# Float64 weight conversion in three VectorE passes; all weight splits on VectorE

## The chip, the cores and the metric

The kernel runs on one core of a Trainium2 chip. The core has TensorE (PE: matmuls into PSUM), VectorE (DVE), ScalarE (ACT), GpSimd (POOL) and SyncE (SP, which here only issues DMAs). Each engine works through its own instructions in order, and semaphores tie the engines together. The metric is device microseconds of one execution; the time of a kernel is the median of its runs.

## The reference

Three stages follow each other on 2304 tokens of width 512. The first is attention with a threshold (4 batches, 8 heads, 576 positions, head width 64). The second is a mixture of eight experts in which each token goes to one expert. The third is a dense layer of width 2048:

```python
def _moe_ref(x, modality_id, w_gate, modality_bias, w1, w2):
    ...
    for e in range(E):                      # E = 8, w1 [8,512,1024], w2 [8,1024,512], float32
        mask = e_idx == e
        h = np.maximum(x[mask] @ w1[e], 0.0)
        out[mask] = gate_w[mask, None] * (h @ w2[e])

def _moe2_ref(x, w_in, w_out):              # w_in [512,2048], w_out [2048,512], float64
    h = x @ w_in
    g = np.maximum(0.01 * h, h)
    return (g @ w_out).astype(np.float32)
```

Only `w_in` and `w_out` matter for the edit itself. They arrive as float64 and the engines compute in float32, so the kernel rebuilds each float32 from the two 32-bit words of a float64. The low word is word 0 of a pair, the high word (sign, exponent, upper mantissa) word 1.

## The kernel before

**Exact products from split operands.** A float32 matrix product is made of three matmuls in a faster format: every operand is split into a high part and the remainder (`hh`, `hl` for activations, `w_3h`, `w_3l` for weights), and high×high, low×high and high×low are added up in PSUM. So each weight block of 128x1024 is split once (`wsplit`, line 1103): ACT copies the rounded high part, and then DVE or POOL subtracts it from the raw block. The argument `on_pool` says which of the two. Before, three of every four splits of expert weights went to POOL, and every second split of the dense layers' weights.

**The expert stage.** The tokens of an expert are gathered in units of 306. Eight units run in a loop (`for u in range(NSTAT)`, line 1362). Unit 0 reads weights called `we`, units 1 to 7 read `w0` to `w6`. A unit has eight steps `g1` (12 matmuls each of 306 columns: one 128-row block of the hidden layer), then eight steps `g2t` (12 matmuls each), and two transposes of the next unit's rows in between. After each `g1` step, ACT writes `hh` (line 1169) and DVE writes `hl` (line 1170) from the step's PSUM tile. Four PSUM tiles (`ps_a`) take turns, so `g1` step f+4 cannot begin before `hl` of step f has been written.

**What fills the steps.** Everything else is hung on steps by the lists `fills[i]`. It is recorded right after step i's matmuls, and it keeps that order on each engine. Splits of the unit's own second-layer weights stand at steps 0, 2, 4, 6 (`SB`), those of the next unit's first-layer weights at 10, 12, 14, 16 (`SA`). A split also lets SP issue the load of the block four splits ahead. The gathers of the unit after next stand at step 13 on POOL.

**Conversions.** There are 16 blocks to convert (`Convert`, line 1114), each 128x1024 values, worked as two halves of 128x512. Each has three parts, `a`, `b` and `c`, placed at steps by `CONV` (line 258): one block in unit 1, three in units 2, 4 and 7, two in units 3, 5 and 6. Part `a` takes the absolute value and clamps (two DVE instructions per half). Part `b` shifts and joins the words (two on DVE) and adds 1 on POOL (integer add). Part `c` shifts back and restores the sign (two on DVE). The first eight blocks are `wi`, the others `cvt`; the raw words are `cv`.

**Dense stage.** It follows after a branch that every engine passes (line 1425). It runs over 9 token blocks of 256. During the first block the last four splits of `wi` and the eight of `wd` (the converted `w_out`, stored to memory and read back) are made, and each `g1` step needs ACT, DVE (line 1175), ACT and DVE (line 1180) after it.

Of the kernel before, what the change touches and what calls it, by code (L numbers as in the profile page):

```python
# [262 lines left out]
HOTS = 0, 2, 4, 6, 8, 10  # L263
# [647 lines left out]
def tile_main(tc, q, k, v, tau, mod, w_gate, bias, w1, w2, w_in, w_out, out):  # L911
    nc = tc.nc
    P = 128
# [4 lines left out]
    V = nc.vector  # L918
    with ExitStack() as ctx:
        c = ctx.enter_context(tc.tile_pool(name="c", bufs=1))  # L920
# [9 lines left out]
        wd = dr.tile([8, P, 1024], F32, name="wd")  # L930
# [17 lines left out]
        onei = c.tile([P, 1], I32, name="onei")  # L948
# [39 lines left out]
        def rest3(_):  # L988
            nc.gpsimd.memset(lst8, 1.0)
            nc.gpsimd.affine_select(out=lst8, in_=lst8, pattern=[[1, 8], [-1, 8]], compare_op=ALU.is_ge, fill=0.0, base=0, channel_multiplier=0)  # L990
            nc.gpsimd.memset(tri, 1.0)
            nc.gpsimd.affine_select(out=tri, in_=tri, pattern=[[1, P]], compare_op=ALU.is_gt, fill=0.0, base=0, channel_multiplier=-1)
            nc.gpsimd.memset(ones, 1.0)
            nc.gpsimd.memset(onei, 1)

        def rest4(_):
            m32 = mod.bitcast(I32).rearrange("(n two) -> n two", two=2)
# [32 lines left out]
        AB, RB, RP, CB = 24, 5, 3, 6  # L1030
        gathers, raws = [], []

        def row_tile(nm):
# [59 lines left out]
        def wtile(nm, tag, dt=F32R):  # L1093
            return (x_tag[0] if tag == "n" else w_p).tile([P, 1024], dt, tag=f"w{tag}", name=nm, bufs=8)
# [12 lines left out]
            return wh, wl  # L1107

        THR_LO = struct.unpack("f", struct.pack("I", 0x38000000))[0]
        THR_HI = struct.unpack("f", struct.pack("I", 0x47EFFFFF))[0]  # L1110

        w_in_f = []

        class Convert:


            def __init__(self, n):
                self.ns = (2 * n, 2 * n + 1)

            def load(self):  # L1120
                self.r, self.t = [], []
                for n in self.ns:
                    ch, hf = divmod(n, 2)
                    raw = cv_p.tile([P, 1024], I32, tag="cvr", name=f"cv{n}", bufs=CB)
                    if ch < 8:
                        src = w_in.bitcast(I32).rearrange("(c p) f -> p c f", p=P)[:, 2 * hf:2 * hf + 2, ch * 512:(ch + 1) * 512]
                        nc.sync.dma_start(out=raw.rearrange("p (c f) -> p c f", c=2), in_=src)
                    else:
                        r0 = ((ch - 8) * 2 + hf) * P
                        nc.sync.dma_start(out=raw, in_=w_out.bitcast(I32)[r0:r0 + P, :])  # L1130
                    self.r.append(raw.rearrange("p (n w) -> p n w", w=2))

            def a(self):
                for n, r in zip(self.ns, self.r):
                    ch, hf = divmod(n, 2)
                    if ch < 8:
                        if hf == 0:
                            w_in_f.append(wtile(f"wi{ch}", "i", F32))
                        t = w_in_f[ch].bitcast(I32)[:, hf * 512:(hf + 1) * 512]
                    else:  # L1140
                        t = cv_p.tile([P, 512], I32, tag="cvt", name=f"cvt{n}", bufs=4)
                    self.t.append(t)
# [12 lines left out]
            def c(self):  # L1155
                for t in self.t:
                    V.tensor_scalar(out=t, in0=t, scalar1=1, scalar2=None, op0=ALU.logical_shift_right)
                for n, t, r in zip(self.ns, self.t, self.r):
                    V.scalar_tensor_tensor(out=t, in0=r[:, :, 1], scalar=-2147483648, in1=t, op0=ALU.bitwise_and, op1=ALU.bitwise_or)
                    ch, hf = divmod(n, 2)  # L1160
                    if ch >= 8:
                        later(6, lambda t=t, ch=ch, hf=hf: nc.sync.dma_start(out=wd[ch - 8, :, hf * 512:(hf + 1) * 512], in_=t.bitcast(F32)))
# [97 lines left out]
        def later(n, fn):  # L1260
            late.append([n, fn])
# [49 lines left out]
        hots = [cv_p.tile([P, 1024], I32, tag="cvr", name=f"hot{k}", bufs=CB) for k in range(3)]  # L1311
        hot_l = [t.bitcast(BF16)[:, 0:9 * P].rearrange("p (j q) -> p j q", q=P) for t in hots[0:2]]
        hot_h = hots[2].bitcast(F16)[:, 0:324].rearrange("p (j q) -> p j q", q=18)
        hot_v = hots[2].bitcast(F16)[:, 324:1620].rearrange("p (j v q) -> p j v q", v=4, q=18)
# [47 lines left out]
        for u in range(NSTAT):  # L1362
# [4 lines left out]
            if u == 0:  # L1367
                for i, fs in LATE.items():
                    for part, a, b in fs:
                        fills[i].extend(chain[part][a:b] if isinstance(chain[part], list) else [chain[part]])  # L1370
                for k, i in enumerate(S0):
                    fills[i].append(lambda k=k: first_w.split(k % 4 != 2))
                for i in range(2):
                    fills[LATE_ROWS[i]].append(lambda i=i: rows.update({i + 1: unit_rows(i)}))
                tr_at = LATE_TR
            else:
                for k, i in enumerate(SB):
                    fills[i].append(lambda k=k: wts[u].split(k % 4 != 2))
                if u == 1:
                    for i, f in zip(HOTS, (lambda: pos_low(0), lambda: pos_low(1), pos_high, lambda: pos_values(0), lambda: pos_values(1))):  # L1380
                        fills[i].append(f)
                    fills[HOTS[5]].append(lambda: step(pos_tables))
                    fills[HOTS[5] + 1].extend(c.load for c in convs[1:CB // 2])
            if not last:
                for k, i in enumerate(SA):
                    fills[i].append(lambda k=k: w_nxt.split(k % 4 != 2))
            if u:
                for ia, ib, ic in CONV.get(u, STG):
                    if cv < 16:
                        c = convs[cv]  # L1390
                        nx = convs[cv + CB // 2] if cv + CB // 2 < 16 else None
# [132 lines left out]
```

## Time and profile before

| what | value |
|---|---|
| median of 3 runs | 1100.1 us (1099.07 to 1100.85) |
| the profiled execution: its time, its span | 1096.98 us, 1095.3 us |
| busy PE, DVE, ACT, POOL over the span | 94%, 68%, 50%, 47% |
| eight expert units | 383.6 to 665.6 us of the span |
| first token block of the dense stage | 673.8 to 704.3 us |
| dense stage, the other eight blocks | until 1078 us |

The profiled execution ran 3.1 us below the median, and its span leaves out 1.7 us of its own time. All times of rows are counted from the start of the span. "Busy" is the time in which an engine has an instruction running, and that includes the time in which the instruction itself is held up. PEclk is the granted clock of TensorE as a share of full speed (2.4 GHz); 0.5 is the lower level, 1.2 GHz.

### The profile page before, as it was taken

Reading aid. Unit: us, or ns where it says so; the run is one execution under the profiler, and the core shown is the slowest. Engines: PE = TensorE matmul, PEld = TensorE weight load, DVE = VectorE, ACT = ScalarE, POOL = GpSimd, SP = SyncE. Lnnn points to the kernel's source line nnn. Section 1 sums busy time; section 2 is a strip of 40 time slices with the busy share of each in tenths; the row PEclk is TensorE's granted clock in tenths of the full one; section 3 lists DMA queues with packets and bytes.
Section 4 is the critical chain, followed back from the end, with each engine's and each line's share of the span. In section 5 each row is a group of like instructions: output and inputs, shape, how many; then the busy total and the mean of one; then the engine's idle time right before and its main releaser. Section 6 shows DMA issues by size and latency. Waiting matters only on the chain. (4 is left out here: it accounts for less than half of the span.)

```text
span 1095.3 us, 19110 instructions
## 1 busy us (share of the span) xinstructions
PE 1025.3 (94%) x6914; PEld 930.6 (85%) x6914; DVE 750.1 (68%) x1525; ACT 546.6 (50%) x1191; POOL 516.2 (47%) x461
## 2 busy tenths in 40 slices
PE   7999999999998889888879877899999999999997
PEld 4788998898897689888879876798989989899896
DVE  7999999999999599699999997822414224132240
ACT  4888888888886244434344334532313324133240
POOL 6688788777876558667777764400000000000000
PEclk9999999999999889989999988999999999999999
DMA  5322324334231285968777843510010100000000
GB/s 132 105 57 59 102 63 99 82 85 100 57 89 23 88 275 157 302 203 241 213 233 255 275 133 117 154 39 30 11 39 1 40 29 11 20 1 20 10 11 20
DMA packets 96264, 109.12 MB, mean 100 GB/s; under 512 B 34448, under 2 KB 74384, under 8 KB 96160
## 3 DMA queue, kind: packets, MB, share of 16 engines
q1 hardware_dynamic: 90880, 98.06, 30.1%
q0 software_dynamic: 5280, 9.75, 2.9%
q8 instruction: 56, 0.92, 0.3%
q14 instruction: 48, 0.39, 0.1%
HBM read 78.47 MB, written 19.96 MB: 90 GB/s over the span
## 5 line engine op out<-in xcount | busy, mean ns | idle before, releaser
L1465 POOL DMA_INDIRECT out<-yo,prow x18 | 17.3, 963 | 366.1 <-ACT yo L1252 366.1
L1175 DVE TENSOR_TENSOR g<-h,g 128x256 f32<-128x256 f32 x144 | 61.0, 424 | 171.7 <-ACT g L1174 171.7
L328 POOL TENSOR_TENSOR Pl<-rw,Ph 128x384 fp32r<-128x384 f32 x115 | 114.5, 1008 | 22.0 <-ACT Ph L323 18.0
L433 ACT ACTIVATE e<-s,mx 128x576 f32<-128x576 f32 x144 | 105.9, 745 | 22.9 <-DVE mx L425 21.7
L425 DVE TENSOR_REDUCE mx<-s 128x1 f32<-128x576 f32 x144 | 106.7, 750 | 14.0 <-PE s L420 10.2
L1174 ACT ACTIVATE g<-h 128x256 f32<-128x256 f32 x144 | 55.4, 385 | 107.0 <-PE h L1215 101.3
L447 DVE SCALAR_TENSOR_TENSOR pp<-s,tb,e 128x576 f32<-128x576 f32 x128 | 102.3, 807 | 4.6 <-ACT e L433 0.7
L1252 ACT ACTIVATE yo<-y,pgate 128x512 f32<-128x512 f32 x18 | 12.4, 688 | 169.8 <-PE y L1233 169.8
L466 PE MATMUL t<-ident,pp 128*128 128x128 f32 x576 | 89.4, 277 | 1.1 <-ACT rw L323 1.0
L420 PE MATMUL s<-kt,qt 128*128 128x288 f32 x256 | 80.5, 330 | 5.4 <-DVE pp L447 2.8
L490 POOL TENSOR_TENSOR Ph<-rw,zz 128x384 fp32r<-128x384 f32 x76 | 76.8, 1010 | 7.1 <-ACT rw L323 5.2
L560 PE MATMUL o<-Ph,hv 128*128 128x320 f32 (+3 forms) x237 | 75.4, 330 | 0.0
L420 PE MATMUL s<-k,qt 128*128 128x288 f32 x256 | 72.2, 296 | 0.0
L466 PEld LDWEIGHTS t<-ident,pp 128*128 128x128 f32 x576 | 67.0, 143 | 4.3 <-ACT rw L323 1.4
L1359 DVE TENSOR_TENSOR xl<-x,xh 128x256 fp32r<-128x256 f32 x36 | 13.0, 421 | 83.8 <-ACT xh L1358 83.8
L561 PE MATMUL o<-Pl,hv 128*128 128x320 f32 (+3 forms) x237 | 68.1, 299 | 0.2 <-POOL Pl L328 0.2
L1169 ACT ACTIVATE hh<-h 128x306 fp32r<-128x306 f32 x64 | 27.2, 427 | 71.2 <-PE h L1215 69.9
L429 DVE TENSOR_TENSOR tb<-mx,taub 128x1 f32<-128x1 f32 x144 | 60.8, 423 | 1.2
L323 ACT ACTIVATE rw<-t 128x384 f32<-128x384 f32 x111 | 54.8, 496 | 10.9 <-PE t L466 10.8
L1252 ACT ACTIVATE yo<-y 128x306 f32<-128x306 f32 x32 | 13.7, 428 | 88.4 <-issue 56.1
L420 PEld LDWEIGHTS s<-kt,qt 128*128 128x128 f32 x256 | 48.6, 190 | 9.3 <-issue 4.1
L560 PEld LDWEIGHTS o<-Ph,hv 128*128 128x128 f32 x237 | 44.9, 189 | 12.2 <-issue 11.9
(591 smaller groups left out, 3681.9 us busy)
## 6 DMA issues: line engine op xcount, KB each, us to landing
k<-kt SPq DMA_DIRECT2D x30, 304.0 KB
cv<-in_moe_w_in SPq DMA_DIRECT2D x16, 512.0 KB
cv<-in_moe_w_out SPq DMA_DIRECT2D x16, 512.0 KB
yt<-yo SPq DMA_DIRECT2D x32, 153.0 KB
x<-yt SPq DMA_DIRECT2D x9, 512.0 KB
rk<-in_k SPq DMA_DIRECT2D x16, 256.0 KB
rq<-in_q SPq DMA_DIRECT2D x16, 256.0 KB
rv<-in_v SPq DMA_DIRECT2D x16, 256.0 KB
```

Of the source, the lines that this page charges most:

```text
L328: fn.tensor_tensor(out=out, in0=a, in1=b.bitcast(F32), op=ALU.subtract)
L420: T.matmul(ps[:, j, 0:288], a, c, start=(m == 0), stop=(m == len(ops) - 1))
L425: V.tensor_reduce(out=mx, in_=get(g, f"s{s}"), op=ALU.min, axis=AX.XY)
L429: V.tensor_tensor(out=tb, in0=get(g, f"mx{s}"), in1=taub, op=ALU.add)
L433: A.activation(out=e, in_=get(g, f"s{s}"), func=AF.Exp, bias=get(g, f"mx{s}"), scale=-1.0)
L447: V.scalar_tensor_tensor(out=p.rearrange("p (a b) -> p a b", a=2), in0=get(g, f"s{s}"), scalar=get(g, f"tb{s}"), in1=get(g, f"e{s}"), op0= ...
L466: T.transpose(ps[:, m * P:(m + 1) * P], p[:, o:o + P], ident)
L490: G.tensor_tensor(out=hi, in0=rw, in1=zz.rearrange("p (a b) -> p a b", a=3), op=ALU.add)
L560: T.matmul(ps[:, a:b], V2[:, vb, :], hi[:, n, a:b], start=(c == 4), stop=False)
L561: T.matmul(ps[:, a:b], V2[:, vb, :], lo[:, n, a:b], start=False, stop=(c == 3))
L1174: nc.scalar.activation(out=g, in_=ps, func=AF.Copy, scale=0.01)
L1175: V.tensor_tensor(out=g, in0=ps, in1=g, op=ALU.max)
```

## The change

A conversion now works on one block of 128x1024. ACT takes the absolute value of the high words and turns the top byte of the low word into a float near 2 in place (`a`). DVE clamps and shifts by 3 in two passes, POOL adds the two words as integers in two halves of 512 (`b`), and DVE restores the sign in one pass (`c`). Each block has one load of 1 MB where there were two of 512 KB, and for `w_out` one store where there were two. All weight splits in the units, and those of `wi` and `wd`, now run on DVE (`on_pool` False). The steps at which parts are placed (`CONV`, `SA`, `SB`) stay as they are. The matmuls and their order on PE do not change.

```diff
             def a(self):
-                for n, r in zip(self.ns, self.r):
...
-                    V.tensor_scalar(out=t, in0=r[:, :, 1], scalar1=0x7FFFFFFF, scalar2=None, op0=ALU.bitwise_and)
-                for t in self.t:
-                    V.tensor_scalar(out=t.bitcast(F32), in0=t.bitcast(F32), scalar1=THR_LO, scalar2=THR_HI, op0=ALU.max, op1=ALU.min)
...
+                    self.t = cv_p.tile([P, 1024], I32, tag="cvt", name=f"cvt{n}", bufs=2)
+                nc.scalar.activation(out=self.t.bitcast(F32), in_=self.w[:, :, 1].bitcast(F32), func=AF.Abs)
+                nc.scalar.activation(out=self.w[:, :, 0].bitcast(F32), in_=self.raw.bitcast(U8).rearrange("p (n b) -> p n b", b=8)[:, :, 3], func=AF.Copy, scale=2.0 ** -27 * (1 + 2.0 ** -9), bias=2.0)

             def b(self):
-                for t in self.t:
-                    V.tensor_scalar(out=t, in0=t, scalar1=0x08000000, scalar2=4, op0=ALU.bitwise_xor, op1=ALU.logical_shift_left)
-                for t, r in zip(self.t, self.r):
-                    V.scalar_tensor_tensor(out=t, in0=r[:, :, 0], scalar=28, in1=t, op0=ALU.logical_shift_right, op1=ALU.bitwise_or)
-                for t in self.t:
-                    nc.gpsimd.tensor_tensor(out=t, in0=t, in1=onei.to_broadcast([P, 512]), op=ALU.add)
+                t = self.t
+                V.scalar_tensor_tensor(out=t.bitcast(F32), in0=t.bitcast(F32), scalar=THR_LO, in1=hit.to_broadcast([P, 1024]), op0=ALU.max, op1=ALU.min)
+                V.scalar_tensor_tensor(out=t, in0=t, scalar=3, in1=zeroi.to_broadcast([P, 1024]), op0=ALU.logical_shift_left, op1=ALU.bitwise_or)
+                for s in (slice(0, 512), slice(512, 1024)):
+                    nc.gpsimd.tensor_tensor(out=t[:, s], in0=t[:, s], in1=self.w[:, s, 0], op=ALU.add)

             def c(self):
-                for t in self.t:
-                    V.tensor_scalar(out=t, in0=t, scalar1=1, scalar2=None, op0=ALU.logical_shift_right)
-                for n, t, r in zip(self.ns, self.t, self.r):
-                    V.scalar_tensor_tensor(out=t, in0=r[:, :, 1], scalar=-2147483648, in1=t, op0=ALU.bitwise_and, op1=ALU.bitwise_or)
...
+                V.scalar_tensor_tensor(out=t, in0=self.w[:, :, 1], scalar=-2147483648, in1=t, op0=ALU.bitwise_and, op1=ALU.bitwise_or)
...
                 for k, i in enumerate(SB):
-                    fills[i].append(lambda k=k: wts[u].split(k % 4 != 2))
+                    fills[i].append(lambda k=k: wts[u].split(False))
...
                 for k, i in enumerate(SA):
-                    fills[i].append(lambda k=k: w_nxt.split(k % 4 != 2))
+                    fills[i].append(lambda k=k: w_nxt.split(False))
...
-                    fills[4 + (3 * k) // 2].insert(0, lambda k=k: moe2_o.split(k % 2))
+                    fills[4 + (3 * k) // 2].insert(0, lambda k=k: moe2_o.split(False))
```

On DVE, this stands before in the first half of unit 5 (its second-layer weights are `w4r`; `cvt_8172` and `cvt_8174` are the two halves of one block):

```order
L1143 TENSOR_SCALAR cvt_8172<-cv_7855 128x512
L1143 TENSOR_SCALAR cvt_8174<-cv_7857 128x512
L1145 TENSOR_SCALAR cvt_8172<-cvt_8172 128x512
L1145 TENSOR_SCALAR cvt_8174<-cvt_8174 128x512
L1170 SCALAR_TENSOR_TENSOR hl<-h,hh 128x306
L1149 TENSOR_SCALAR cvt_8172<-cvt_8172 128x512
L1149 TENSOR_SCALAR cvt_8174<-cvt_8174 128x512
L1151 SCALAR_TENSOR_TENSOR cvt_8172<-cv_7855,cvt_8172 128x512
L1151 SCALAR_TENSOR_TENSOR cvt_8174<-cv_7857,cvt_8174 128x512
L1170 SCALAR_TENSOR_TENSOR hl<-h,hh 128x306 x3
```

Of the change, the same place on DVE (the same block is `cvt_8085`, and line numbers are those of the changed file):

```order
L1109 TENSOR_TENSOR w_4l<-w4r_7925,w_4h 128x1024
L1161 SCALAR_TENSOR_TENSOR hl<-h,hh 128x306
L1144 SCALAR_TENSOR_TENSOR cvt_8085<-cvt_8085,hit 128x1024
L1145 SCALAR_TENSOR_TENSOR cvt_8085<-cvt_8085,zeroi 128x1024
L1161 SCALAR_TENSOR_TENSOR hl<-h,hh 128x306
L1109 TENSOR_TENSOR w_5l<-w4r_7970,w_5h 128x1024
L1161 SCALAR_TENSOR_TENSOR hl<-h,hh 128x306 x2
L1109 TENSOR_TENSOR w_6l<-w4r_8014,w_6h 128x1024
L1151 SCALAR_TENSOR_TENSOR cvt_8085<-cv_7789,cvt_8085 128x1024
L1161 SCALAR_TENSOR_TENSOR hl<-h,hh 128x306 x2
```

Between the first and the third `hl` of the unit there stood four conversion instructions on halves; now there are two on a whole block and one split.

On POOL, this stands before at the turn from unit 4 to unit 5 (`xg` are the gathers, line 1106 the splits):

```order
L1044 DMA xg_0_8074<-x_dram,tab 102x512
L1044 DMA xg_1_8076<-x_dram,tab 102x512
L1044 DMA xg_2_8078<-x_dram,tab 102x512
L1106 TENSOR_TENSOR w_3l<-w4r_7902,w_3h 128x1024
L1106 TENSOR_TENSOR w_4l<-w4r_7997,w_4h 128x1024
L1153 TENSOR_TENSOR cvt_8172<-cvt_8172,onei 128x512
L1153 TENSOR_TENSOR cvt_8174<-cvt_8174,onei 128x512
L1106 TENSOR_TENSOR w_5l<-w4r_8050,w_5h 128x1024
L1106 TENSOR_TENSOR w_7l<-w4r_8138,w_7h 128x1024
```

Of the change, the same place on POOL:

```order
L1147 TENSOR_TENSOR cvt_7951<-cvt_7951,cv_7633 128x512 x2
L1047 DMA xg_0_7992<-x_dram,tab 102x512
L1047 DMA xg_1_7994<-x_dram,tab 102x512
L1047 DMA xg_2_7996<-x_dram,tab 102x512
L1147 TENSOR_TENSOR cvt_8085<-cvt_8085,cv_7789 128x512 x2
L1147 TENSOR_TENSOR cvt_8306<-cvt_8306,cv_7928 128x512 x2
```

Only the adds and the gathers are left there.

On ACT, this stands before in the first half of unit 5:

```order
L1105 ACTIVATE w_4h<-w4r_7997 128x1024
L1169 ACTIVATE hh<-h 128x306 x2
L1105 ACTIVATE w_5h<-w4r_8050 128x1024
L1169 ACTIVATE hh<-h 128x306 x2
L1105 ACTIVATE w_6h<-w4r_8096 128x1024
```

Of the change, the same place on ACT:

```order
L1108 ACTIVATE w_4h<-w4r_7925 128x1024
L1139 ACTIVATE cvt_8085<-cv_7789 128x1024
L1140 ACTIVATE cv_7789<-cv_7789 128x1024
L1160 ACTIVATE hh<-h 128x306 x2
L1108 ACTIVATE w_5h<-w4r_7970 128x1024
```

The two new passes stand between the copy of a weight block and the first `hh` of the unit.

## Rows read from the trace of the kernel before

**Rows 1.** The page: busy time of each engine, share of the span, instructions.
```profile
PE 1025.3 (94%) x6914; PEld 930.6 (85%) x6914; DVE 750.1 (68%) x1525; ACT 546.6 (50%) x1191; POOL 516.2 (47%) x461
```

**Rows 2.** Windows: stretch, length, busy PE, PEld, DVE, ACT, POOL, PEclk, DMA share, GB/s.
```profile
383.60:421.10 37.50, 34.09 (x231) 32.67 (x231) 33.13 (x77) 17.57 (x30) 23.85 (x14) 0.91 0.79 249
421.10:665.60 244.50, 213.85 (x1436) 208.40 (x1434) 231.34 (x296) 97.14 (x165) 172.98 (x88) 0.94 0.70 221
524.14:560.64 36.50, 30.72 (x206) 29.96 (x205) 36.50 (x50) 14.09 (x24) 25.72 (x15) 0.95 0.75 236
595.96:629.39 33.43, 30.47 (x206) 30.02 (x205) 33.00 (x39) 14.02 (x24) 25.03 (x14) 0.95 0.82 260
629.39:665.60 36.21, 30.43 (x194) 29.08 (x192) 35.12 (x48) 12.71 (x20) 22.68 (x12) 0.91 0.39 124
665.60:704.30 38.70, 26.63 (x197) 25.21 (x197) 30.63 (x39) 21.64 (x44) 15.64 (x7) 0.91 0.42 141
```

**Rows 3.** Waits of PE in units 1 to 7: total us, times, longest us.
```profile
PE h L1215 <- DVE hl L1170: 16.7, 9, 5.1
PE y L1245 <- DVE hl L1170: 14.0, 8, 3.4
```

**Rows 4.** Timeline around the longest of these waits, unit 5: start, us, engine, instruction.
```profile
566.67 5.68 DVE L1149 TENSOR_SCALAR cvt<-cvt 128x512 int32<-128x512 int32 x1
567.37 2.40 POOL L1106 TENSOR_TENSOR w_3l<-w4r,w_3h 128x1024 fp32r<-128x1024 f32 x1
569.70 2.36 POOL L1106 TENSOR_TENSOR w_4l<-w4r,w_4h 128x1024 fp32r<-128x1024 f32 x1
...
574.21 0.46 DVE L1170 SCALAR_TENSOR_TENSOR hl<-h,hh 128x306 fp32r<-128x306 f32 x1
...
574.34 0.62 PE L1215 MATMUL h<-xh,w_2h 128*128 128x306 f32 x1 [5.07 <-DVE hl L1170]
```

**Rows 5.** Windows of two half units without a PE gap (first half, second half).
```profile
455.65:469.88 14.23, 14.23 (x105) 14.23 (x103) 10.19 (x11) 7.26 (x13) 12.37 (x7) 1.00 0.82 232
581.50:595.96 14.46, 14.46 (x105) 14.22 (x104) 14.03 (x21) 6.61 (x12) 8.20 (x5) 1.00 0.81 284
```

**Rows 6.** Windows, lines 1143, 1145, 1149, 1151, 1157, 1159 (DVE), 1106 (DVE, POOL).
```profile
421.10:665.60 244.50, 21.33 (x32) 0.94 0.70 221
421.10:665.60 244.50, 12.74 (x32) 0.94 0.70 221
421.10:665.60 244.50, 45.10 (x32) 0.94 0.70 221
421.10:665.60 244.50, 20.47 (x32) 0.94 0.70 221
421.10:665.60 244.50, 48.35 (x31) 0.94 0.70 221
421.10:665.60 244.50, 23.62 (x30) 0.94 0.70 221
421.10:665.60 244.50, 26.56 (x16) 109.18 (x41) 0.94 0.70 221
```

**Rows 7.** Single lines: one instruction's ns, min/median/max.
```profile
L1149 DVE TENSOR_SCALAR cvt<-cvt x16: 409/414/5721, 558.0 to 661.3; 128x512 int32<-128x512 int32 x16
L1153 POOL TENSOR_TENSOR cvt<-cvt,onei x16: 1028/1422/2557, 559.4 to 665.0; 128x512 int32<-128x512 int32 x16
```

**Rows 8.** Timeline: a split on ACT, the same on DVE, and what follows it.
```profile
684.21 1.07 ACT L1105 ACTIVATE wi_6h<-wi 128x1024 fp32r<-128x1024 f32 x1
...
687.64 1.22 DVE L1106 TENSOR_TENSOR wi_6l<-wi,wi_6h 128x1024 fp32r<-128x1024 f32 x1
688.78 0.41 DVE L1175 TENSOR_TENSOR g<-h,g 128x256 f32<-128x256 f32 x1
```

**Rows 9.** Timeline from the last unit to the dense stage, and its first block.
```profile
668.67 0.68 DVE L1159 SCALAR_TENSOR_TENSOR cvt<-cv,cvt 128x512 int32<-128x512 int32 x1
...
673.33 0.42 ACT L1358 ACTIVATE xh<-x 128x256 fp32r<-128x256 f32 x1 [7.18 <-DVEq L1425]
...
681.92 2.12 DVE L1180 TENSOR_TENSOR hl<-g,hh 128x256 fp32r<-128x256 f32 x1
```

More of the change, by code (lines that the diff above doesn't have):

```diff
@@ L12 @@
 I32 = mybir.dt.int32
+U8 = mybir.dt.uint8
 BF16 = mybir.dt.bfloat16
@@ L947, in tile_main @@
         ones = c1.tile([P, P], BF16, name="ones")
-        onei = c.tile([P, 1], I32, name="onei")
+        zeroi = c.tile([P, 1], I32, name="zeroi")
+        hit = c.tile([P, 1], F32, name="hit")
         mt = ca_p.tile([P, 18, 2], I32, name="mt")
@@ L993, in rest3 @@
             nc.gpsimd.memset(ones, 1.0)
-            nc.gpsimd.memset(onei, 1)
+            nc.gpsimd.memset(zeroi, 0)
+            nc.gpsimd.memset(hit, struct.unpack("f", struct.pack("I", 0x47EFFFFF))[0])
         def rest4(_):
@@ L1029, in tile_main @@
         prow = c.tile([P, 18], I32, name="prow")
-        AB, RB, RP, CB = 24, 5, 3, 6
+        AB, RB, RP, CB = 24, 5, 3, 3
         gathers, raws = [], []
@@ L1117, in __init__ @@
             def __init__(self, n):
-                self.ns = (2 * n, 2 * n + 1)
+                self.n = n
             def load(self):
[L1121 to L1131, printed above, removed]
@@ L1133, in a @@
-            def a(self):
-                for n, r in zip(self.ns, self.r):
[L1135 to L1142, printed above, removed]
-                    V.tensor_scalar(out=t, in0=r[:, :, 1], scalar1=0x7FFFFFFF, scalar2=None, op0=ALU.bitwise_and)
-                for t in self.t:
-                    V.tensor_scalar(out=t.bitcast(F32), in0=t.bitcast(F32), scalar1=THR_LO, scalar2=THR_HI, op0=ALU.max, op1=ALU.min)
@@ L1155, in c @@
-            def c(self):
-                for t in self.t:
-                    V.tensor_scalar(out=t, in0=t, scalar1=1, scalar2=None, op0=ALU.logical_shift_right)
-                for n, t, r in zip(self.ns, self.t, self.r):
-                    V.scalar_tensor_tensor(out=t, in0=r[:, :, 1], scalar=-2147483648, in1=t, op0=ALU.bitwise_and, op1=ALU.bitwise_or)
-                    ch, hf = divmod(n, 2)
-                    if ch >= 8:
-                        later(6, lambda t=t, ch=ch, hf=hf: nc.sync.dma_start(out=wd[ch - 8, :, hf * 512:(hf + 1) * 512], in_=t.bitcast(F32)))
+                n = self.n
@@ new lines, in load @@
+                self.raw = raw = cv_p.tile([P, 2048], I32, tag="cvr", name=f"cv{n}", bufs=CB)
+                if n < 8:
+                    nc.sync.dma_start(out=raw.rearrange("p (c f) -> p c f", c=4), in_=w_in.bitcast(I32).rearrange("(c p) f -> p c f", p=P)[:, :, n * 512:(n + 1) * 512])
+                else:
+                    nc.sync.dma_start(out=raw.rearrange("p (c f) -> p c f", c=2), in_=w_out.bitcast(I32).rearrange("(c p) f -> p c f", p=P)[:, 2 * n - 16:2 * n - 14, :])
+                self.w = raw.rearrange("p (n w) -> p n w", w=2)
@@ new lines, in a @@
+            def a(self):
+                n = self.n
+                if n < 8:
+                    w_in_f.append(wtile(f"wi{n}", "i", F32))
+                    self.t = w_in_f[n].bitcast(I32)
+                else:
+                    self.t = cv_p.tile([P, 1024], I32, tag="cvt", name=f"cvt{n}", bufs=2)
+                nc.scalar.activation(out=self.t.bitcast(F32), in_=self.w[:, :, 1].bitcast(F32), func=AF.Abs)
+                nc.scalar.activation(out=self.w[:, :, 0].bitcast(F32), in_=self.raw.bitcast(U8).rearrange("p (n b) -> p n b", b=8)[:, :, 3], func=AF.Copy, scale=2.0 ** -27 * (1 + 2.0 ** -9), bias=2.0)
@@ L1164, in unit_rows @@
+            def c(self):
+                n, t = self.n, self.t
+                V.scalar_tensor_tensor(out=t, in0=self.w[:, :, 1], scalar=-2147483648, in1=t, op0=ALU.bitwise_and, op1=ALU.bitwise_or)
+                if n >= 8:
+                    later(6, lambda: nc.sync.dma_start(out=wd[n - 8], in_=t.bitcast(F32)))
         def unit_rows(u):
@@ L1310, in tile_main @@
         cv = 0
[L1311 to L1314, printed above, removed]
+        hots = [cv_p.tile([P, 2048], I32, tag="cvr", name=f"hot{k}", bufs=CB) for k in range(2)]
+        hot_l = [hots[0].bitcast(BF16)[:, 2048 * k:2048 * k + 9 * P].rearrange("p (j q) -> p j q", q=P) for k in range(2)]
+        hot_h = hots[1].bitcast(F16)[:, 0:324].rearrange("p (j q) -> p j q", q=18)
+        hot_v = hots[1].bitcast(F16)[:, 324:1620].rearrange("p (j v q) -> p j v q", v=4, q=18)
         def pos_low(k):
@@ L1347, in split_in @@
         def split_in(k):
-            moe2_i.append(wsplit(w_in_f[k], f"wi_{k}", "ab"[k // 4], k % 2))
+            moe2_i.append(wsplit(w_in_f[k], f"wi_{k}", "ab"[k // 4], False))
         def tok_load(m, pool, tag, n):
-            x = pool.tile([P, 1024], F32, tag=tag, name=f"x{m}", bufs=n)
+            x = pool.tile([P, 2048 if tag == "cvr" else 1024], F32, tag=tag, name=f"x{m}", bufs=n)[:, 0:1024]
             nc.sync.dma_start(out=x.rearrange("p (c n) -> p c n", c=4), in_=yt[:, m * 256:(m + 1) * 256].rearrange("(c p) n -> p c n", p=P))
@@ L1382, in tile_main @@
                     fills[HOTS[5]].append(lambda: step(pos_tables))
-                    fills[HOTS[5] + 1].extend(c.load for c in convs[1:CB // 2])
+                    fills[HOTS[5] + 1].extend(c.load for c in convs[1:CB])
             if not last:
                 for k, i in enumerate(SA):
-                    fills[i].append(lambda k=k: w_nxt.split(k % 4 != 2))
+                    fills[i].append(lambda k=k: w_nxt.split(False))
             if u:
@@ L1390, in tile_main @@
                         c = convs[cv]
-                        nx = convs[cv + CB // 2] if cv + CB // 2 < 16 else None
+                        nx = convs[cv + CB] if cv + CB < 16 else None
                         fills[max(ia, 0)].append(c.a)
```

1 line of the change is left out of this document (removed).

## The prediction

> **What bounds the kernel now.** I begin with the page's busy shares. PE runs 94% of the span [rows 1], but a share over three stages says nothing about one of them, so the next view is the windows, cut where a unit's first matmul starts [rows 2]. The seven units from 421.1 to 665.6 us take 244.5 us. DVE is busy for 231.3 of them (95%) and PE for 213.9, while PE's granted clock averages 0.94. In unit 4 (524.1 to 560.6) DVE is busy for all 36.5 us. PE, at 94% of the whole kernel, is therefore not what ends last here.
>
> PE's waits name the instruction it waits for: 16.7 + 14.0 = 30.7 us in these units, every one of them for `hl` from DVE [rows 3]. The timeline of the longest shows why `hl` is late [rows 4]. A `tensor_scalar` of line 1149, half a block, lasts 5.68 us there, where its median is 0.414 us [rows 7]. Meanwhile POOL works through two splits, 2.40 and 2.36 us. The DVE instruction does not end before the second POOL split has. Three `hl` stand behind it, all four PSUM tiles are full, and PE stops for 5.07 us. Such waits cost more than their length: a granted clock of 0.94 over the seven units [rows 2] is about an eighth of the time at the lower of the two levels (1.2 GHz), and the matmul after this wait shows 0.62 us.
>
> How short could a unit be? A first half without a PE gap takes 14.23 us, a second half 14.46 us [rows 5]: 28.69 us. The last unit has no transposes of a next one, about 0.9 us less. Six units and the last are 6 x 28.69 + 27.75 = 199.9 us. Against 244.5 that leaves 44.6 us, which is the 30.7 us of waits plus what the low clock and ragged restarts cost. This is the most that the change can win in these units.
>
> **What the change removes from DVE there.** Six lines disappear: 21.33 + 12.74 + 45.10 + 20.47 + 48.35 + 23.62 = 171.6 us [rows 6]. Lines 1149 and 1157 alone are 93.5 us for 63 instructions, 1.48 us each where 0.414 is the median: over two thirds of that is being held up by POOL. The 16 splits that DVE already makes cost 26.56 us (1.66 each), also held up; without that a split takes 1.22 us and the next instruction starts after 1.14 [rows 8].
>
> **What it adds to DVE.** The 41 splits that POOL makes in these units (109.2 us of POOL) come over, so 57 splits at 1.14 are 65.0 us. Three passes of 1024 for 16 blocks are 48 instructions. No such pass is in the trace. Below they are bounded by two halves in the short form of line 1149 (0.83 us), above by two of line 1159 (1.36, from 0.68 [rows 9]). I take 1.14, the split, since it too is 1024 wide with two inputs: 54.7 us. DVE's sum is 231.3 - 171.6 - 26.6 + 65.0 + 54.7 = 152.8 us, or 76% of 199.9. With the bounds it is 138 to 163. DVE stops being the engine that ends last on average.
>
> **What is left of the stalls.** A mean of 76% hides bunches. In the first half of a unit with three blocks DVE has four splits, four first passes, one last pass (9 x 1.14), eight `hl` and two `xl` (10 x 0.39): 14.2 us against PE's 14.23, plus one add of about 1.2 us that a split may have to wait for. It ends some 1.2 us late, of which the second `g2t` step, where the late `hl` are first needed, forgives most. That is so in units 2, 4 and 7; the other first halves carry two passes less. I leave 1 us per unit, plus 1 us for the table of positions in unit 1: 8 us. Gain in the seven units: 44.6 - 8 = 36.6 us.
>
> **The adds and POOL.** 32 adds stay, 1.03 us at the least and 1.42 in the median [rows 7]. Their second input is now every other word of the raw block instead of one broadcast word, a case that no row shows. Below I keep 1.03; above I take twice the median, 2.84, as if the skipped words were read too. I take 1.2.
>
> **ACT.** Two passes per block are new, 32 in all. As a weight copy of the same width they cost 1.07 us [rows 8]; above, 2.14, if the skipped words count. ACT goes from 97.1 to 131 us of 200. Queued behind a block's passes are the unit's first `hh`. They begin 3.2 us into the unit instead of 1.7, but `hl` of step 0 is needed only by step 4, at about 6.8 us, so I cost this at nothing. The cover is gone when a pass takes over 2.4 us. In unit 7 the third block's pass also waits for the store of the first block; behind it stand only `yo`, which have a PSUM tile of slack.
>
> **SP and the queues.** 16 loads of 1 MB replace 32 of 512 KB and 8 stores replace 16, in the same places of SP's order. Loads of weights no longer wait for POOL's subtraction but for DVE's. Cost: nothing while the DMA engines keep up (a rival, below).
>
> **Unit 0.** DVE is busy for 33.1 of 37.5 us [rows 2] with routing arithmetic; it gains eight splits (9 us) and loses POOL's hold-ups. I take 0, bounds -5 and +4.
>
> **The turn to the dense stage.** DVE's last conversion ends at 668.67 + 0.68 = 669.35 or, with its second half, near 669.95. ACT has been idle since 673.33 - 7.18 = 666.15 and starts when the branch is passed [rows 9]. With DVE in time, those 3.8 us go.
>
> **The first dense block.** `hl` there reads two inputs from SBUF and shows 2.12 us beside a POOL split [rows 9], against 0.41 for a neighbour of the same size [rows 8]; five such hold-ups are about 9 us of DVE. Five splits come over (5 x 1.14 = 5.7). ACT and DVE take turns here, so not all of the 3.3 us reaches PE: 2.5 us.
>
> **Sum.** 36.6 + 0 + 3.8 + 2.5 = 42.9 us off the profiled execution's 1096.98: 1054.1. The median stands 3.1 us above that execution, and I carry this over: **1057 us**.
>
> **A rule beside the rows.** The splits, the three passes and the old line 1159 all take two inputs from SBUF. Line 1159 averages 23.62 / 30 = 0.79 us against 0.68 alone [rows 6, 9], so such instructions are held up too, if less than line 1149. The Trainium skill, "SBUF — State Buffer", section "Who interferes with whom", says that a VectorE instruction with two SBUF inputs contends with a GpSimd instruction that reads SBUF, that the pair of ports is an exclusive lock, and that whoever issues first blocks the other entirely. The trace agrees: 5.68 us in place of 0.414 for as long as POOL's splits ran. By this rule the new DVE work stays exposed to all 32 adds; by the rows alone it would mostly run free.
>
> **Rivals.**
> *The remaining adds hold DVE up each time.* For: every new DVE instruction has two SBUF inputs, and line 1159 shows hold-ups. Against: POOL falls from 173 us to some 60, so there is little left to meet. With each add holding DVE for 1.2 us, a block costs 2.4 us more and DVE reaches 152.8 + 38 = 191 us of 200. The first halves of three-block units then overrun by about 4 us each, with the clock's loss, 15 us: 1072.
> *The DMA engines become the bound.* Unit 6 already has them at 0.82 and 260 GB/s in 33.4 us; at 28.7 us the same bytes need 303 GB/s. If 260 is the most that a whole unit gets, units 1 to 6 (221 x 244.5 - 124 x 36.21 = 49.5 MB) take 190 us instead of 172, and the gain is 18 us smaller: 1075. Against: 260 / 0.82 leaves room up to 317, and the second half in [rows 5] ran at 284 with no PE gap.
> *ACT's passes hold up `hh`.* If a pass that reads bytes or every other word costs 3.5 us, ten first halves or so lose 2.2 us each: 1079. It decides from 2.4 us on.
> *The adds are slow, and it ends slower than before.* If reading every other word makes an add take 4 us, DVE stands behind two of them per block: 152.8 + 16 x 8 = 281 us in the units, 36 more than before, less the 6 us won elsewhere: 1130. It decides from about 3.1 us per add ((244.5 + 6 - 152.8) / 32), just above my upper bound of 2.84.
>
> **Chances.** PE-bound units with small stalls 0.60; adds hold DVE up 0.13; DMA-bound 0.14; ACT late 0.06; slow adds 0.07. Low end: no stall is left and unit 0 wins its 5 us, 1057 - 8 - 5 = 1044. High end: the DMA and hold-up cases with a few us of their own, 1080. What lies outside is the slow adds, the worst of ACT and the tails. A change of 0.2% (2.2 us) is about what can be told from none here. Faster 0.90, same 0.03, slower 0.07 (the slow adds, with a little of ACT).
>
> **What would show it.** Right: in the units DVE busy falls to 70 to 85%, PE's waits for `hl` drop from 30.7 us below 10, unit lengths come to 29 to 31 us, the clock stays near 1.0, no DVE instruction of 1024 exceeds 2.5 us, and DVE is done before PE at the turn. Wrong: an add over 2 us, an ACT pass over 2 us, PE waits that end on ACT or on a weight load (DMA share near 1.0), or units still above 32 us.

## The result and the profile after

The changed kernel takes 1068.16 us (median of 4 runs, 1066.87 to 1074.27), against 1099.59 us for the kernel before beside it. The ratio is 0.9728, 95% interval 0.971 to 0.9746. The forecast was 1057 (1044 to 1080): right in direction and inside the range, with a gain of 31.4 us where 42.9 were summed up. The profiled execution took 1068.17 us (span 1066.4), 28.8 us less than the one before (1096.98); the times of stages below are from these two.

The page's busy shares of the changed kernel, beside [rows 1]:

```profile
PE 1016.3 (95%) x6914; PEld 922.3 (86%) x6914; DVE 677.8 (64%) x1431; ACT 576.4 (54%) x1223; POOL 400.6 (38%) x412
```

Windows of the changed kernel, columns as in [rows 2]: unit 0, units 1 to 7, the last unit, the first layer of the first dense block, and the end of unit 0.

```profile
384.57:426.17 41.60, 35.99 (x231) 34.19 (x231) 30.42 (x80) 17.54 (x30) 20.36 (x12) 0.88 0.84 254
426.17:646.41 220.24, 203.73 (x1436) 199.51 (x1434) 168.22 (x193) 127.22 (x197) 79.28 (x47) 0.99 0.76 240
...
613.44:646.41 32.97, 29.43 (x194) 28.60 (x192) 25.22 (x26) 18.39 (x26) 11.17 (x8) 0.95 0.43 136
...
651.04:677.96 26.92, 25.83 (x193) 25.11 (x193) 21.89 (x40) 19.63 (x41) 0.00 (x0) 0.91 0.47 159
...
414.27:426.17 11.90, 9.30 (x51) 8.92 (x49) 3.01 (x6) 3.73 (x7) 1.52 (x2) 0.71 0.76 197
```

Units 1 to 7 went from 244.5 to 220.2 us, DVE in them from 231.3 to 168.2 (76%), and the granted clock from 0.94 to 0.99. Waits of PE there, beside [rows 3]:

```profile
PE h L1206 <- DVE hl L1161: 6.8, 9, 2.0
PE xT L1188 <- DMA xg<-x_dram,tab: 6.1, 4, 2.0
PE y L1236 <- DVE hl L1161: 3.7, 2, 2.9
```

The 30.7 us of waits for `hl` have become 10.5. In the middle stands a wait that the kernel before did not have in its list: the transposes wait for gathered rows. The timelines of POOL and of PE around one such wait (unit 6 begins at 582.29):

```profile
580.73 3.37 POOL L1147 TENSOR_TENSOR cvt<-cvt,cv 128x512 int32<-128x512 int32 x2 [16.92 <-ACT w_3h L1108]
584.28 2.07 POOL L1047 DMA_INDIRECT xg<-x_dram,tab  x1 [0.18 <-PE h L1206]
586.66 1.95 POOL L1047 DMA_INDIRECT xg<-x_dram,tab  x1 [0.31 <-issue]
588.91 1.22 POOL L1047 DMA_INDIRECT xg<-x_dram,tab  x1 [0.30 <-issue]
...
599.02 0.39 PE L1188 MATMUL xT<-ident,xg 102*128 102x102 f32 x2 [1.51 <-DMA xg<-x_dram,tab]
```

The gathers belong to step 13 of unit 5, but on POOL they stand behind the adds of that unit's last block, and these run at the unit's very end. So the rows are asked for 2 to 7 us into unit 6, whose transposes come 14.7 us into it. Before, the same gathers were not much earlier (unit 6 begins there at 595.96):

```profile
596.47 1.12 POOL L1044 DMA_INDIRECT xg<-x_dram,tab  x1 [0.18 <-issue]
597.90 1.21 POOL L1044 DMA_INDIRECT xg<-x_dram,tab  x1 [0.31 <-issue]
599.41 1.22 POOL L1044 DMA_INDIRECT xg<-x_dram,tab  x1 [0.31 <-issue]
...
614.39 0.69 PE L1197 MATMUL xT<-ident,xg 102*128 102x102 f32 x6
```

They began 0.5 to 3.5 us into the unit, but the transposes came only 18.4 us into it, so nothing waited. After the change the transposes come 3.7 us sooner, the first gather starts 1.5 us later, and two of the three issues last 2.0 us instead of 1.2; why they do was not traced. The new operations, min/median/max ns:

```profile
L1147 POOL TENSOR_TENSOR cvt<-cvt,cv x16: 1300/1316/2272, 550.4 to 644.3; 128x512 int32<-128x512 int32 x16
...
L1145 DVE SCALAR_TENSOR_TENSOR cvt<-cvt,zeroi x8: 1224/1226/1226, 549.0 to 640.8; 128x1024 int32<-128x1024 int32 x8
...
L1140 ACT ACTIVATE cv<-cv x16: 1129/1158/1198, 428.7 to 636.2; 128x1024 f32<-128x1024 uint8 x16
```

Neither the passes on DVE nor those on ACT are held up. An add takes 1.3 us, and 2.2 to 2.3 where it meets DVE, as one half of most blocks does. Elsewhere: the gap at the turn is 4.63 us (8.17 before, from the starts and ends of matmuls), the first layer of the first dense block 26.92 (29.56), unit 0 4.1 us longer, and all that follows that layer 3.4 us shorter, which nothing in the change seems to explain. With 24.3 us in units 1 to 7, and all that comes ahead of unit 0 1.0 us longer, these add up to the 28.8. (Ahead of the prediction that layer is called the first token block. The whole block lasted from 673.80 to 725.75, and the last matmul of the stage ended at 1088.94, not at 1078.)

### The profile page after: what moved, and what is told of

Same layout as the page of the kernel before. It is cut to its first block, busy times and chain, and to the rows that moved or that the text cites. A ratio compares the mean times of both kernels' runs of the same rounds, so it can differ in the third digit from the quotient of the medians.

```text
span 1066.4 us, 18948 instructions
## 1 busy us (share of the span) xinstructions
PE 1016.3 (95%) x6914; PEld 922.3 (86%) x6914; DVE 677.8 (64%) x1431; ACT 576.4 (54%) x1223; POOL 400.6 (38%) x412
## 5 line engine op out<-in xcount | busy, mean ns | idle before, releaser
L1147 POOL TENSOR_TENSOR wi<-wi,cv 128x512 int32<-128x512 int32 x16 | 26.2, 1656 | 81.1 <-ACT w_3h L1108 25.6
L1147 POOL TENSOR_TENSOR cvt<-cvt,cv 128x512 int32<-128x512 int32 x16 | 26.7, 1688 | 65.1 <-ACT w_3h L1108 43.2
```

## Experiments

**Which half of the change is it?** My theory going in: the removed VectorE passes are the larger part, the splits' move the smaller. The rival: POOL's splits held VectorE up, and their move is the gain. Two kernels do one half each.

`conv_only`, the changed kernel with

```diff
-moe2_i.append(wsplit(w_in_f[k], f"wi_{k}", "ab"[k // 4], False))
+moe2_i.append(wsplit(w_in_f[k], f"wi_{k}", "ab"[k // 4], k % 2))
-wts[u].split(False)
+wts[u].split(k % 4 != 2)
-w_nxt.split(False)
+w_nxt.split(k % 4 != 2)
-moe2_o.split(False)
+moe2_o.split(k % 2)
```

> The changed kernel with the weight splits back on GpSimd where the kernel before had them: only the conversion is new. Theory (VectorE's removed passes are the larger part of the gain, and splits on GpSimd still stretch what VectorE runs beside them): 1080, 1074 to 1088, with new passes of 1.22 us that reach 3 to 5 us beside a split, and TensorE's waits for hl between 10 and 25 us in units 1 to 7. Rival (the splits on GpSimd are what held VectorE up): 1090 or more.

Measured: 1096.11 us, ratio 0.9977 (0.9951 to 1.0003). My theory fell. Units 1 to 7 and PE's waits in them:

```profile
423.40:667.50 244.10, 215.85 (x1436) 208.50 (x1434) 170.41 (x154) 127.04 (x198) 187.16 (x89) 0.94 0.71 221
...
PE y L1236 <- DVE hl L1161: 15.6, 8, 3.9
PE y L1237 <- POOL w_5l L1109: 4.7, 4, 2.0
PE h L1206 <- DVE hl L1161: 4.6, 6, 1.6
PE xT L1188 <- DMA xg<-x_dram,tab: 2.2, 3, 1.1
```

DVE's busy time fell by 61 us and the units still take 244.1. The waits for `hl` went from 30.7 to 20.2 us, but 4.7 us of waits for POOL's own splits of `w_5` and 2.2 us for gathered rows have come in. The timeline of one wait in unit 4 shows what busy time doesn't:

```profile
533.96 2.40 POOL L1109 TENSOR_TENSOR w_3l<-w3r,w_3h 128x1024 fp32r<-128x1024 f32 x1
534.35 12.59 DVE L1109 TENSOR_TENSOR w_6l<-w3r,w_6h 128x1024 fp32r<-128x1024 f32 x1 [0.40 <-ACT w_6h L1108]
536.31 2.40 POOL L1109 TENSOR_TENSOR w_4l<-w3r,w_4h 128x1024 fp32r<-128x1024 f32 x1
538.67 2.55 POOL L1147 TENSOR_TENSOR wi<-wi,cv 128x512 int32<-128x512 int32 x2
541.19 2.36 POOL L1109 TENSOR_TENSOR w_5l<-w3r,w_5h 128x1024 fp32r<-128x1024 f32 x1
543.51 2.35 POOL L1109 TENSOR_TENSOR w_7l<-w3r,w_7h 128x1024 fp32r<-128x1024 f32 x1
...
548.00 0.85 DVE L1161 SCALAR_TENSOR_TENSOR hl<-h,hh 128x306 fp32r<-128x306 f32 x2
548.52 0.62 PE L1236 MATMUL y<-hl,w_6h 128*128 128x306 f32 x1 [3.94 <-DVE hl L1161]
```

A split that takes 1.22 us alone starts 0.39 us after a POOL split and ends 1.08 us after POOL's sixth instruction in a row, 12.59 us later. With fewer passes, DVE meets the same POOL work with other instructions. So long a hold-up is the exception: of the 29 DVE instructions in these units that took at least 0.3 us longer than alone, this is the only one that was kept out for more than one POOL instruction.

`splits_only`, the kernel before with the opposite edit in the same four places, and the seven passes kept:

```diff
-w_nxt.split(k % 4 != 2)
+w_nxt.split(False)
...
```

> The kernel before with all weight splits that the change moves on VectorE, and the old conversion of seven passes. Theory: VectorE's sum in units 1 to 7 goes up by about 28 splits of 1.22 us less what its long passes lose beside GpSimd, so it stays at 225 to 260 us of some 240; TensorE goes on waiting 25 us or more for hl and the time is 1085 to 1110. Rival (the splits on GpSimd are what held VectorE up): the passes fall to their alone time, and the time is 1078 or less.

Measured: 1069.48 us, ratio 0.9717 (0.9697 to 0.9737), not to be told from the whole change. Units 1 to 7, PE's waits, and line 1149 of [rows 7] in this kernel:

```profile
428.56:644.93 216.37, 206.16 (x1436) 202.17 (x1434) 193.95 (x338) 96.71 (x165) 74.62 (x47) 0.98 0.77 244
...
PE y L1245 <- DVE hl L1170: 6.2, 3, 2.6
PE h L1215 <- DVE hl L1170: 3.9, 4, 2.0
...
L1149 DVE TENSOR_SCALAR cvt<-cvt x16: 410/419/427, 549.3 to 638.2; 128x512 int32<-128x512 int32 x16
```

DVE took over 41 splits (50 us at 1.22) and its busy time fell from 231.3 to 194 us: of the 231.3, some 87 were hold-ups by this estimate (231.3 - (194 - 50)). The longest line 1149 went from 5.72 us to 0.43. VectorE at 90% of the units leaves PE waiting 10.1 us for `hl`, no more than the changed kernel at 76%.

**Where do 3.4 us in the dense stage come from?** From the second block's first matmul to the ninth's are seven blocks: (1043.40 - 725.75) / 7 = 45.38 us before, (1014.97 - 700.25) / 7 = 44.96 after. The change also swaps one 4-byte tile (`onei`) for two (`zeroi`, `hit`); in the compiled program each has a slot of 32 bytes, and the tiles of weights behind it lie 32 bytes further on. `pad_only` is the kernel before with

```diff
+        hit = c.tile([P, 1], F32, name="hit")
...
+            nc.gpsimd.memset(hit, 0)
```

> The kernel before with one more unused tile of 4 bytes in each partition, in the pool where the change adds one: nothing else. It asks why a dense block takes 44.96 us in the changed kernel and 45.38 before, with the matmuls of 256 columns 117.8 ns apart instead of 120.1 and those of 512 columns alike. Theory (the pace goes with where the later tiles lie in SBUF, which the extra tile shifts): the blocks take 44.96 and the time falls by some 3.5 us, to 1093 in the profiled run. Rival (it comes from elsewhere): 45.38 as before and no change.

Measured: ratio 0.9966 (0.9953 to 0.9978), dense blocks of 44.93 us ((1044.31 - 729.81) / 7). So the place of the weights in SBUF is worth 3.7 us; its profiled execution, 1097.48 us, was the slowest of its runs. `splits_only`, with the old place, has blocks of 45.39, and `conv_only`, with the new one, 44.92. This bears on both: the 0.23% of `conv_only` are no more than the 0.34% that the place alone is worth, so its conversion gained nothing. And at the same place `splits_only` would be ahead of the whole change, by some 5 us, give or take 3, as an estimate from the ratios (0.9728 - 0.9717 + 0.0034). Its units 1 to 7 take 216.4 us against 220.2, with no wait for rows in them: in the change as it was made, the new conversion seems to have cost time.

`x_moved` is the next kernel, `gather_early`, with a 32-byte pool of its own ahead of the dense stage's pool. It moves the activations and `wd` by 32 bytes and leaves `wi`:

```diff
+        pad = ctx.enter_context(tc.tile_pool(name="pad", bufs=1, reuse_waits="tile", side="right"))
+        nc.gpsimd.memset(pad.tile([P, 8], F32, tag="pad", name="pad"), 0.0)
         x_tag[:] = ctx.enter_context(tc.tile_pool(name="xp", ...
```

> The changed kernel with the gathers at step 5 (1063.0, dense blocks of 44.96 us), and with the tiles of the dense stage's own pool, the activations among them, moved by 32 bytes; the weights of the first matmul stay. The unused 4-byte tile moved the weights by 32 bytes and left the activations; the matmuls of 256 columns went from 120.0 to 117.8 ns apart. Theory 1 (where the weights lie decides): 117.8 ns still, same time. Theory 2 (weights and activations at the same distance from a multiple of 64 bytes is what is fast): 120.0 ns again, blocks of 45.4 us and 3.5 us more.

Measured: 1063.83 us, blocks of 44.71 us ((1009.66 - 696.71) / 7), the 256-column matmuls 116.7 ns apart. Theory 2 falls, and theory 1 does not say why it is faster still. Why 32 bytes matter stays open. The gain of 0.25 us per block did not show in the total, which is that of `gather_early` (1062.99 us) within the interval.

**The late gathers.** `gather_early`, the changed kernel with

```diff
-                    fills[13].append(lambda: rows.update({u + 2: unit_rows(u + 1)}))
+                    fills[5].append(lambda: rows.update({u + 2: unit_rows(u + 1)}))
```

> The changed kernel with the three row gathers of the unit after next issued at step 5 of a unit instead of step 13, ahead of the adds of the unit's last block. Theory: in the changed kernel the gathers stand on GpSimd behind adds that run only at the end of a unit, so they are issued 2 to 7 us into the next unit and land too late for its transposes (TensorE waits 6.1 us for them in units 1 to 7). Early, those waits go to under 1 us and the time falls from 1068.2 to 1060 to 1064; unit 0's gather wait (2.6 us) and the waits for hl (10.5 us) stay. Rival (the DMA queues are the bound): the rows just come later or the weight loads do, ScalarE's waits for weights grow over 10 us, and the time stays at 1066 to 1070.

Measured: 1062.99 us, ratio 0.9674 (0.9654 to 0.9694), below the changed kernel's interval. As expected, the waits for rows in units 1 to 7 are gone; what is left of PE's waits there, under their window:

```profile
423.63:638.69 215.06, 205.34 (x1436) 202.10 (x1434) 168.54 (x194) 127.29 (x197) 74.99 (x47) 0.98 0.78 247
...
PE h L1206 <- DVE hl L1161: 5.3, 7, 2.0
PE y L1236 <- DVE hl L1161: 4.3, 3, 2.9
```

**What the new conversion is worth.** `splits_early` is `splits_only` with the same early gathers and the unused tile, so that only the conversion differs from `gather_early`.

> The old conversion of seven passes, with all the moved splits on VectorE, the row gathers at step 5 and the unused tile of 4 bytes: all that helped so far, without the new conversion. It asks what the new conversion is worth once nothing else is in the way (the same with the new conversion measured 1063.0, ratio 0.9674). Theory: with no long GpSimd work beside it VectorE carries the old passes too (194 us of 216 in units 1 to 7), so 1061 to 1066. Rival (at 90 per cent VectorE is the bound again, and the new conversion pays once gathers come in time): 1068 or more, with waits for hl over 15 us.

Measured: 1064.56 us, ratio 0.9697 (0.967 to 0.9723): 0.23% behind `gather_early`, with intervals that overlap. Units 1 to 7 take 215.9 us there and 215.1 with the new conversion. The same pair on another schedule (`tuned_old` makes the edits of `tuned`, below, in `splits_early`) gives 0.9681 (0.9668 to 0.9694) against 0.9669 (0.9656 to 0.9683). In the profiled executions of this pair units 1 to 7 take the same, 213.1 and 213.0 us. Three passes instead of seven are worth 1 to 3 us here, at the edge of what can be told.

> The same schedule as the candidate with the new conversion, but with the old conversion of seven passes (and the unused tile of 4 bytes). It asks with a finer measurement what the new conversion is worth once the splits are off GpSimd. Theory (its VectorE passes now fit beside TensorE, apart from a longer second half): 1 to 4 us more than the candidate. Rival (VectorE at 90 per cent is the bound): 8 us more or worse. Other rival: no difference within 1 us.

**What the adds cost.** In the kernels with the new conversion the split of `w_5` meets the first block's adds. Timeline of the changed kernel:

```profile
590.32 0.47 DVE L1161 SCALAR_TENSOR_TENSOR hl<-h,hh 128x306 fp32r<-128x306 f32 x1
590.63 3.54 POOL L1147 TENSOR_TENSOR cvt<-cvt,cv 128x512 int32<-128x512 int32 x2 [0.51 <-issue]
590.71 2.31 DVE L1109 TENSOR_TENSOR w_5l<-w5r,w_5h 128x1024 fp32r<-128x1024 f32 x1
592.95 0.85 DVE L1161 SCALAR_TENSOR_TENSOR hl<-h,hh 128x306 fp32r<-128x306 f32 x2
```

The split starts 0.08 us after the first add and ends 1.09 us after that add has; the second add, which follows the first without a gap, lasts 2.27 us instead of 1.31. So here DVE does get in between two POOL instructions, and holds up the second.

`no_add` is `gather_early` without the adds (and with an exclusive or in the second pass):

```diff
-                for s in (slice(0, 512), slice(512, 1024)):
-                    nc.gpsimd.tensor_tensor(out=t[:, s], in0=t[:, s], in1=self.w[:, s, 0], op=ALU.add)
```

> The changed kernel with the gathers at step 5 and without GpSimd's integer adds (the second pass on VectorE puts in the offset by an exclusive or, so the weights lose their last three bits). It prices the adds: what they hold up on VectorE, over gathers that come in time. Theory of the prediction's first rival (the adds hold VectorE up each time): the split of w_5 falls from 2.2 us to 1.22, TensorE's wait of 0.6 us at step 7 of six units goes away, and the time falls by 3 us or more, to 1060 or less. Rival: the adds are beside the path, 1061.5 to 1064 as with gathers at step 5 alone.

Measured: 1064.21 us, no gain. The `w_5l` do take 1.22 us, and unit 1 takes 29.05 us instead of 32.69. But in units 2 and 5 another wait comes instead. ACT in unit 2, behind a store of the unit's results:

```profile
461.80 0.43 ACT L1241 ACTIVATE yo<-y 128x306 f32<-128x306 f32 x1 [8.62 <-DMA yt<-yo]
462.12 1.05 ACT L1108 ACTIVATE w_4h<-w1r 128x1024 fp32r<-128x1024 f32 x1
```

The DMA engines moved 353 GB/s from 455 to 462 us, ACT could not reuse its output tile, and PE then waited 4.1 us for `hl`. After it the granted clock is 0.73 for 8.9 us. So what the adds alone cost is not shown: the store came late in the same run.

**Candidates.** `first_on_dve` puts unit 0's own splits on VectorE too, on top of `gather_early`:

```diff
-first_w.split(k % 4 != 2)
+first_w.split(False)
```

> The changed kernel with the gathers at step 5 and with the first unit's own splits on VectorE too, which the change leaves on GpSimd. Theory (a split on GpSimd holds up what VectorE runs beside it, so unit 0 gains as the others did): the routing operations of unit 0 fall to their alone time, TensorE's wait of 2.9 us for the one-hot goes, and unit 0 takes 35 to 37.5 us instead of 38.8; 1060 to 1062. Rival (VectorE is busy 98 per cent of unit 0's first part and five splits of 1.2 us more make it later): unit 0 takes 39 to 43 and the time is 1064 or more.

Measured: 1061.49 us, ratio 0.9665 (0.9635 to 0.9695), not to be told from `gather_early`. The 2.9 us wait for the one-hot goes, and 3.5 us of waits for gathered rows stand in its place (0.6 before): unit 0 takes 37.8 us instead of 38.7.

`shifted` changes two table entries on top of `gather_early`:

```diff
-CONV = {1: STG[0:1], 2: STG3, 4: STG3, 7: STG3}
+CONV = {1: STG[0:1], 2: STG3, 4: STG3, 6: STG3}
-LATE_ROWS, LATE_TR = (9, 12), 13
+LATE_ROWS, LATE_TR = (9, 16), 13
```

> A candidate: the changed kernel with the gathers at step 5, the third block of conversion of the last unit done in the last but one, and the second set of gathers of unit 0 at step 16 instead of 12. Theory: unit 7's wait of 2.9 us for hl goes and unit 6 hides the block (VectorE 26 of 29.4 us), and the gathers for unit 1 land sooner: 1058 to 1061. Rival: unit 6 becomes as late as unit 7 was and the time stays at 1062 to 1064.

Measured: 1064.97 us. Unit 6 waits 3.3 us for `hl` where unit 7 did, and unit 0 still waits 3.1 us for rows, so that the second set of gathers is not what delays the first.

`tuned` starts from `first_on_dve`:

```diff
-STG3 = ((-1, 1, 4), (4, 6, 10), (11, 13, 15))
+STG3 = ((-1, 1, 4), (4, 9, 11), (11, 13, 15))
-CONV = {1: STG[0:1], ...
+CONV = {1: ((-1, 9, 12),), ...
```

> A candidate, with the new conversion: gathers at step 5, the first unit's splits on VectorE, and the middle passes of two kinds of blocks moved to the second half of a unit, where no hl waits behind them (unit 1's block from steps 1 and 4 to 9 and 12, the second block of units 2, 4 and 7 from steps 6 and 10 to 9 and 11). Theory (what is left in units 1 to 7 are hl that stand on VectorE behind a pass or behind a split that the adds hold up): unit 1's wait of 2.0 us, unit 7's of 3.3 and the two of 0.74 go, each with the low clock that follows the long ones, and the time is 1053 to 1057. Rival (the passes then hold up the evacuation of the transposes and the gains are given back): 1060 or more.

Measured: 1062.51 us. Unit 1 takes 28.9 us, but unit 2 takes 35.5 behind a store that was 7.8 us late, and the turn grows from 4.6 to 7.8 us because the last block ends later. `three_early` moves the third block of unit 7 to unit 3, on top of `first_on_dve`:

```diff
-CONV = {1: STG[0:1], 2: STG3, 4: STG3, 7: STG3}
+CONV = {1: STG[0:1], 2: STG3, 3: STG3, 4: STG3}
```

> A last candidate: gathers at step 5, the first unit's splits on VectorE, and the third block of conversion of unit 7 done in unit 3, so that the last unit has two blocks and no middle one. Theory (unit 7's wait of 2.9 to 3.3 us for hl goes with the low clock behind it, and unit 3 pays 0.8 us as units 2 and 4 do; the turn to the dense stage gets no longer): 1057 to 1060. Rival (the conversion's loads come one unit sooner, and the weights' loads or the units' stores wait behind them as in the other schedules that were tried): 1061 or more.

Measured: 1064.44 us. Unit 7's wait is gone; in unit 5 ACT waits for another store, and PE 6.1 us for what comes after it:

```profile
558.00 1.12 ACT L1139 ACTIVATE cvt<-cv 128x1024 f32<-128x1024 f32 x1 [7.20 <-DMA wd<-cvt]
```

Every schedule that takes a wait on VectorE away ends at 1061 to 1065. `gather_early`, one number changed, beats both kernels; nothing further could be told from it.

## Why the prediction was right in direction and 11 us too good

**The reading of the kernel before** was right: waits for `hl`, late because POOL's splits hold VectorE up. So was the sign of the whole. Of the signs named for being right, DVE's share (76%) and the clock (0.99) came; the waits for `hl` (10.5 us, not below 10), the unit lengths (30.2 to 33.0 us, not 29 to 31) and VectorE's end at the turn did not. One sign of being wrong came too, an add of over 2 us.

**"What the change removes from DVE there"** is the step whose reason failed. The two edits were put into one sum of VectorE's time, 171.6 us of passes at its head, as though that sum set the time. `conv_only` takes the passes away and gains nothing; `splits_only` keeps them and gains everything. The sum did not tell these apart, because a busy time with 87 us of hold-ups in it is not work. The right sign is in part luck: with the conversion alone the same sum is 231.3 - 171.6 + 54.7 = 114.4 us, which would have called VectorE free, and `conv_only` gained nothing. By these runs what counts is which POOL work VectorE meets, and how much stands behind what it starts there.

**DVE's sum**: 152.8 us forecast (138 to 163), 168.2 measured. Passes at 1.22 us instead of 1.14 are 3.9 us, splits at 1.22 another 4.6, and the seven `w_5l` held up by 1 us each 7: together the 15.4 that were missing.

**"What is left of the stalls", 8 us**, was the mis-sized term: 220.2 - 199.9 = 20.3 us. Of it, 6.1 us are waits for rows, a queue that the prediction passed over. The order on POOL shown ahead of it has the gathers right behind two adds, and they already began inside the next unit before; it was the slow first half of that unit that hid them. A forecast of shorter units had to ask whether the rows would still be in time. `gather_early` took the 6.1 us away and 5.2 us off the units. Another 10.5 us are waits for `hl`: 2.0 in unit 1, 2.2 in unit 2, 2.9 in a late `g2t` step of the last unit, 0.6 to 1.0 elsewhere. The remaining 3.7 us were not taken apart; the clock of 0.99 is in them.

**Unit 0** was put at 0 and lost 4.1 us, at the bound. The count was wrong: its own splits stay on POOL, and only three for the next unit moved. The loss is its end, 11.9 us for 6.2, with waits of 2.6 us for rows and a granted clock of 0.71. The same work before, columns as in [rows 2]:

```profile
414.90:421.10 6.20, 6.20 (x50) 6.20 (x48) 4.66 (x4) 3.72 (x7) 4.62 (x3) 1.00 0.67 201
```

Kernels with the same unit 0 took from 38.7 us to 43.8; what sets the landing of its rows stays open.

**The turn** (3.8 forecast, 3.54 measured) and **the first dense block** (2.5, 2.64) were right in size. At the turn the forecast had VectorE done before PE, and it was not: its last split ends at 647.99, 1.6 us after the last unit. But ACT, whose wait there ended on VectorE's sequencer before [rows 9], now waits for its own:

```profile
650.57 1.34 ACT L1349 ACTIVATE xh<-x 128x256 fp32r<-128x256 f32 x4 [3.64 <-ACTq L1416]
```

**Not in the sum at all**: 3.4 us in the rest of the dense stage, from the weights' place in SBUF (`pad_only`).

**The rivals.** The adds do hold VectorE up, about once per unit and not at each of the 32, and `no_add` shows no net price, with a late store in its way. The DMA engines were not the bound at 260 GB/s: unit 5 of `gather_early` ran 29.1 us at 309 GB/s. Whether they are next is not shown: `no_add`, `tuned` and `three_early` were stopped by late stores, but while ACT waited the engines moved 353 GB/s in the first and 240 GB/s in the last. ACT's passes (1.16 us) and the adds (1.30 to 2.28) stayed under their thresholds. The Trainium skill, "SBUF — State Buffer", section "Who interferes with whom", has the pair of ports locked for a whole instruction, and lets issue order decide who blocks. Most hold-ups here agree, such as that of `w_5l` by one add (2.31 us for 1.22). The 12.59 us, over six POOL instructions, go further, and so do the 5.68 us that the prediction took as agreeing: they span a gather and two splits. What makes VectorE miss its turn in these cases stays open.

## What to carry to other kernels

Before you add up an engine's busy time, compare each line's median with its longest: what is held up is not work, and removing instructions from such an engine can gain nothing, as `conv_only` did. When a change has two parts, forecast each alone, and look at what stands behind each moved or delayed instruction on every queue, the gathers among them. And when all work of one kind gets faster by a constant, check whether a tile has moved in memory before you look for a mechanism.

## What the runs showed of the hardware that was not expected

- A VectorE split of 1.22 us beside six GpSimd instructions in a row lasted 12.59 us (`conv_only`). Beside two adds in a row the same kind of split got in after the first and lasted 2.31 us (the changed kernel).
- One unused tile of 4 bytes, in a slot of 32, changed the distance of 256-column matmuls from 120.0 to 117.8 ns (`pad_only`); with the activations and `wd` moved by 32 bytes as well it was 116.7 (`x_moved`). Those of 512 columns stayed between 232.4 and 232.8.
- After PE's wait of 4.1 us in `no_add` came 8.9 us at a mean granted clock of 0.73: as an estimate, another 2.4 us (0.27 x 8.9) on top of the wait.
- Row gathers that GpSimd issues took 1.1 to 1.2 us each in units 3 to 6 before, and the first two of three took 1.9 to 2.1 us after the change.
